# Linear attention ahead of an MLP: chunks of 64 tokens on zero-padded heads, a quartered array for the first batch, and a new order of work

## The chip, the core and the metric

The kernel runs on one core of a Trainium2 chip. The metric is the device time of one execution in microseconds. The engines are TensorE (PE; PEld is its weight load), VectorE (DVE), ScalarE (ACT), GpSimd (POOL) and SyncE (SP), which issues most DMAs.

## What is computed

A linear attention with decay over blocks of 64 tokens, then a two-layer MLP on its result. Shapes: 4 batches, 8 heads, 768 tokens, head size 64; the MLP goes from 512 to 2048 and back for 3072 tokens.

```python
for b in range(nb):                      # blocks of 64 tokens
    intra = einsum('bhic,bhjc->bhij', qb, kb) * Dmask        # lam**(i-j), i >= j
    intra = einsum('bhij,bhjd->bhid', intra, vb)
    inter = einsum('bhid,bhde->bhie', qb * lam_pow, kv_state)
    out[:, :, sl] = intra + inter
    kv_state = lam_block * kv_state + einsum('bhsd,bhse->bhde', kb * rev_pow, vb)
x = out.transpose(0, 2, 1, 3).reshape(B * S, H * D)
h = x @ w_in
g = where(h >= 1, h, where(h <= -1, 0, (h + 1) ** 2 / 4))
return g @ w_out
```

The block size may be chosen freely as long as the decay is carried along; the result is the same recurrence.

## The kernel before

The 3072 tokens are cut into eight stripes, (batch, first block of 128, number of blocks):

```python
STRIPES = [(0, 0, 4), (0, 4, 2), (1, 0, 3), (1, 3, 3), (2, 0, 3), (2, 3, 3), (3, 0, 3), (3, 3, 3)]
FORMS = "pfffwwww"
```

A stripe has four units, one for each pair of heads; L02v is the load of v for stripe 0, pair 2. Attention works in chunks of 128 tokens. A unit's work on TensorE is: transposes of k and q (T and Q, L344), scores of k against q (S, L368 or L372), k against v for the state (R, L449 or L455), and the output from masked scores and from the state before (O, L506, L513, L519, L527, L532, L538). DVE applies the mask (s, L383 or L389) and carries the state (r: a scan, L468, or step by step, L475 and L477). ScalarE, POOL and DVE cast and scale k, q and v (L295 to L320) and ScalarE evacuates PSUM (t, u, o).

The letter in FORMS says how two heads of 64 share the 128 x 128 array. In "p" (stripe 0) a matmul takes half or a quarter of the array for one head. In "f" (stripes 1 to 3) k and v lie beside zeros, kz and vc, so that the state comes out block-diagonal; scores take half the rows. In "w" (stripes 4 to 7) k is zero-padded per head, k and q are transposed by a DMA issued from SyncE (L336), and the output comes with tokens on the partitions and is transposed by another DMA (X, L557).

The MLP of a stripe is 16 tiles of the first layer (P, or K for the first three of stripe 0, one slice of the contraction at a time as soon as its pair of heads is there; L595, L609), ScalarE's ReLU (h, L618), the rest of the activation on DVE in groups of four tiles (A, L575 to L577), the second layer in four parts for each 128 rows (Y, L627), a copy (y) and a store (U). The last 128 rows are closed in two column parts (Z, L647). The weights come in eight casting DMAs issued from POOL (W0 to W7, L235 and L239).

The order of all this is written out in one string of words, ORDER. Every engine and every DMA queue executes its instructions in that order; a word such as `W0@L00q` makes a load wait for another. D1 is a dummy matmul on the identity (L583). The list before has 23 of them in the start.

Of the kernel before, what the change touches and what calls it, by code (L numbers as in the profile page):

```python
# [16 lines left out]
def _ins(ap, idx, mid):  # L17

    a = list(ap.ap)
    a = a[:idx] + [[0, mid]] + a[idx:]  # L20
    return bass.AP(ap.tensor, ap.offset, a)

FORMS = "pfffwwww"
STRIPES = [(0, 0, 4), (0, 4, 2), (1, 0, 3), (1, 3, 3), (2, 0, 3), (2, 3, 3), (3, 0, 3), (3, 3, 3)]

ORDER = """
D1 L00q D1 B0a D1 B2a D1 D1 L01q q01d D1 L03q D1 L00k L01k D1 D1 L01v D1 q00d B1a L00v D1 D1
k00a D1 D1 k01g D1 T00 Q01 T01 D1 E t00 Q00 L02k v01a u00 D1 q03d R01 D1 r01 k02g L02q D1 B3a
# [5 lines left out]
W6@L10v t11 S10 P0c L20k@W1 q13d r11 R10 h0e Q12 h0d s10 T12 S11 r10 t12 u12 s11 P0f z13a O11  # L40
S12 o11 O10 A01 z12g T13 h0c Q13 W7@L02q Y010 h0f t13 u13 h0a Y020 v12g L20q@W1 q20g Y030 Y021
s12 Y000 Y011 o10 L20v@W1 Y031 v13a A02 k21g Y001 Y022 Y032 S13 Y012 R13 A03 k20a Y013 R12
L21q@W1 b13d r13 s13 y01 z20g Y033 O13 r12 O12 y03 o13 Y023 o12 T20 P12 Y002 L21k@W7 v20g y02
Q20 q21g h12 u20 t20 P15 L30k h15 R20 P13 P10 Q21 h13 h10 u21 S20 P11 q23g P17 T21 h11 h17 r20
P16 s20 P1b t21 v21d O20 z21d k22a P14 o20 q22d R21 A10 r21 h1b L30q h14 h16 Y003 L21v z22g Q22
S21 k23g s21 P19 P1d y00 P1a T22 z23g k30g h19 A11 h1a u22 P1f T30 t22 q30g z30g L31k L31q k31g
L31v h1f U01 z31g P18 q31g Q30 P1c U00 t30 S22 Q23 h1d T23 u30 s22 P1e t23 Y100 Y101 h18 u23 A12
G40 h1c v23g T31 S23 s23 k33g v22g v33g Q31 O21 Y110 t31 o21 u31 R22 L30v Y111 v32g R23 h1e r22
r23 Y112 S30 z33d A13 q33g O22 O23 o22 s30 o23 Y102 P21 P27 h27 L40k Q33 T33 R33 Y113 u33 t33
k32g r33 P23 q32d S31 L40q y11 v31d v30g P22 R31 T32 Q32 Y103 h22 u32 t32 L40v z32g r31 P24 s31  # L50
G41 R30 R32 G42 k42g k40g h21 h23 P20 r30 S32 r32 s32 h20 h24 P25 P2a A20 q40d P29 O30 k41g h2a
y10 P2b S33 P28 O32 h2b h29 P2e o30 h28 P2c h2c s33 q41d h25 O31 A22 P26 h26 o31 P2d P2f o32 O33
Y200 h2d o33 L50q P33 h2f h2e P32 h33 P30 P31 A21 Y201 h30 T40 T41 h32 G43 P39 A23 h31 v42a v41d
Y202 P38 P3a A30 h39 q42a U03 h3a P37 R42 h37 S40 Y210 v40d L50k s40 P35 R40 r42 Y211 h38 q51g
Y203 k43a P3b G50 R41 S41 y20 r40 h3b T42 v43d h35 q43g P3c k51d s41 L50v U11 q50a U20 r41 Y212
P34 O40 T43 O41 k50g Y213 U02 o40 S42 v50a P3f h34 v52g T50 X40 k52g y21 P3e R43 P3d s42 h3c o41
L60q P36 r43 S43 q53a O42 h3e Y320 h36 Y220 s43 o42 h3f A31 T51 O43 o43 Y221 R52 S50 v51a A32
Y300 Y222 h3d k53g X41 r52 Y301 X42 Y321 Y223 X43 R50 Y302 q52d Y322 P43 R51 A33 y22 P42 Y303
s50 r51 Y323 S51 v53g U10 T53 T52 r50 h43 y32 s51 L60k P47 q62g P40 O51 h42 P4a h40 S52 k60g
L60v o51 O50 h47 h4a s52 y30 q60a P4b R53 P41 P46 S53 r53 h41 q61a P45 Y310 h45 Y311 U22 k61a  # L60
k63d A40 P44 h4b O52 v62g P48 s53 q63g o50 U30 h46 h44 P49 O53 h48 P4d T60 o52 X51 T61 X50 v63a
v60g o53 P4c X52 h4c X53 Y312 Y313 S60 P4f k62d v61g y31 P4e R60 h49 Y410 A41 s60 U32 h4e Y400
A42 r60 h4d R62 h4f P53 Y411 A43 T62 r62 T63 h53 Y401 L70q q71g Y402 q73g q70g S61 U31 P51 h51
P5a Y403 Y420 R63 y40 Y421 P54 h54 s61 S62 R61 r61 r63 s62 h5a Y412 P56 L70k h56 O60 P52 L70v
U40 Y413 k70d P50 O62 h52 o60 v70g y41 k71g P5b U41 P59 h50 h5b h59 O61 P55 o61 S63 T70 P58 A50
P57 X61 Y422 h57 s63 O63 v72d h55 Y423 P5d h58 o63 k72a P5f P5c v71d A51 h5d P5e X60 o62 X63 A52
R70 R71 S70 y42 h5c Y500 Y501 X62 P61 h5f h5e T71 q72g v73g r70 P63 h63 h61 Y510 U42 T72 P62 P65
A53 R72 Y502 h65 s70 r71 P60 Y503 h62 P64 Y511 h60 k73a r72 Y512 P6d Y513 h64 S71 y50 R73 h6d
P67 A60 s71 P68 r73 O71 P6a S72 O70 o71 y51 T73 h67 s72 h68 P66 P69 h6a O72 P6b X71 S73 P6e h69
P6c s73 o70 h66 h6b Y520 U21 A62 O73 o72 X72 h6c Y521 X70 o73 A61 P6f h6f X73 Y522 Y610 Y600  # L70
Y601 Y523 h6e P70 Y611 y52 P73 h73 Y602 P72 Y612 h70 A63 P71 Y603 Y613 h71 P76 y60 h72 P79 U50
y61 h79 P78 P75 P77 h78 h75 U52 h77 P74 A70 P7d h76 P7b h74 P7a P7e h7b h7a U51 A71 h7e Y620 P7f
# [5 lines left out]
def order(ns):  # L78
    return ORDER.split()
# [663 lines left out]
```

## Time and profile before

| | us |
|---|---|
| median of 3 runs (lowest, highest) | 220.63 (220.22, 220.96) |
| span of the profiled execution | 219.9 |
| TensorE busy in it | 209.4 |
| DVE, ACT, POOL busy | 148.9, 125.4, 60.9 |

The profiled execution has no other time than its span; the runs are timed without a profile. In the time line a row gives the start, the length of a merged group, the engine, line, operation, operands and count; a matmul's length contains its way through the array, so that the distance between two starts is what it costs in a row of others.

### The profile page before, as it was taken

The numbers are of one execution on the slowest core, as the hardware profiler recorded it, in microseconds if no ns is written. First come the engines' busy times: TensorE is split into PE (matmuls) and PEld (weight loads), VectorE is DVE, ScalarE is ACT, GpSimd is POOL, SyncE is SP. The second block draws the span as 40 slices with busy tenths as digits, with TensorE's granted clock in tenths as the row PEclk, the third lists the DMA queues.
The fourth block names the chain that finished last, engine by engine and source line by source line (L and its number), as shares of the span: only waits on it lengthen the run. The fifth ranks groups of instructions, "written<-read, shape, count | busy, mean of one in ns | idle before, by whom it ended". The sixth has DMA issues, their size and how long they took to land.

```text
span 219.9 us, 4417 instructions
## 1 busy us (share of the span) xinstructions
PE 209.4 (95%) x1667; PEld 121.0 (55%) x1667; DVE 148.9 (68%) x239; ACT 125.4 (57%) x268; POOL 60.9 (28%) x122
## 2 busy tenths in 40 slices
PE   7488999999998999999999999999999999999994
PEld 2246445446765566555655666456655565555443
DVE  1387177971998789998499489936898649346700
ACT  3675689327983576874832686326655383256320
POOL 4376036007499810430311045003600000000000
PEclk9999999999999999999999999999999999999999
DMA  4999999999999993849999999899944222310103
GB/s 123 238 233 203 206 215 191 176 221 219 232 276 231 214 192 74 206 84 255 165 202 163 167 256 151 164 243 224 210 96 97 54 66 57 145 74 23 50 22 121
DMA packets 100629, 35.95 MB, mean 163 GB/s; under 512 B 89216, under 2 KB 97664, under 8 KB 100608
## 3 DMA queue, kind: packets, MB, share of 16 engines
q1 hardware_dynamic: 96384, 31.47, 69.0%
q0 software_dynamic: 4224, 4.19, 12.2%
q8 instruction: 13, 0.21, 0.4%
q14 instruction: 8, 0.07, 0.1%
HBM read 27.27 MB, written 6.29 MB: 153 GB/s over the span
## 4 chain that ended last, share of the span: by engine, by line
PE 85%; SPq 5%; DMA 5%; ACT 2%; issue 1%; POOL 1%; DVE 0%; DVEq 0%; ACTq 0%
PE ph L595 36%; PE py L627 34%; SPq L164 3%; DMA v_nat<-in_v_dram 3%; PE ps L368 2%; DMA xT<-xn 2%; PE pk L449 2%; PE py L647 2%; PE po L506 2%; PE pt L344 1%; PE ps L372 1%; PE ph L609 1%; PE po L513 1%; PE po L532 1%; SPq L166 1%; SPq L160 1%
## 5 line engine op out<-in xcount | busy, mean ns | idle before, releaser
L618 ACT ACTIVATE tt<-ph,one 128x384 bf16<-128x384 f32 (+2 forms) x128 | 70.5, 584 | 41.1 <-PE ph L595 29.5
L595 PE MATMUL ph<-xT,w_in_sb 128*128 128x384 bf16 (+2 forms) x500 | 93.1, 325 | 0.5 <-DMA xT<-xn 0.5
L627 PE MATMUL py<-w_out_sb,gT 128*128 128x512 bf16 x368 | 87.7, 379 | 0.0
L595 PEld LDWEIGHTS <-w_in_sb 128*128 128x128 bf16 x500 | 46.5, 98 | 30.5 <-issue 0.2
L627 PEld LDWEIGHTS <-gT 128*128 128x128 bf16 x368 | 34.5, 98 | 35.0 <-DVE sz L477 0.8
L389 DVE TENSOR_TENSOR sc<-ps,mask 128x768 bf16<-128x768 f32 (+1 forms) x28 | 25.6, 914 | 11.9 <-PE ps L368 11.6
L576 DVE TENSOR_TENSOR tt<-tt,mm 128x1536 bf16<-128x1536 bf16 (+2 forms) x32 | 32.6, 1019 | 1.1
L577 DVE TENSOR_TENSOR gT<-tt,mm 128x1536 bf16<-128x1536 bf16 (+2 forms) x32 | 32.0, 998 | 1.2
L575 DVE TENSOR_SCALAR mm<-tt 128x1536 bf16<-128x1536 bf16 (+2 forms) x32 | 19.7, 616 | 18.5 <-ACT tt L618 17.7
L315 POOL TENSOR_SCALAR kq<-k_nat,dec 128x192 bf16<-128x192 f32 (+2 forms) x36 | 19.6, 556 | 24.9 <-DMA k_nat<-in_k_dram 24.8
L635 ACT COPY osb<-py 128x512 f32<-128x512 f32 x23 | 13.5, 585 | 20.4 <-PE py L627 16.0
L320 POOL TENSOR_TENSOR kq<-q_nat,dec 128x384 bf16<-128x384 f32 (+1 forms) x15 | 13.2, 891 | 28.5 <-DMA q_nat<-in_q_dram 15.2
L477 DVE SCALAR_TENSOR_TENSOR sz<-sz,lam_blk,pk 128x128 bf16<-128x128 bf16 x48 | 16.4, 347 | 3.5 <-PE pk L449 2.2
L297 POOL CAST vc<-v_nat 128x384 bf16<-128x384 f32 (+1 forms) x15 | 9.3, 629 | 31.6 <-DMA v_nat<-in_v_dram 15.6
L344 PE MATMUL pt<-ident,kq 128*128 128x128 bf16 x96 | 9.4, 220 | 3.2 <-ACT kq L311 2.4
L548 ACT CAST xn<-po 128x384 bf16<-128x384 f32 x16 | 7.7, 478 | 5.3 <-PE po L532 5.2
L550 ACT CAST xT<-po 128x384 bf16<-128x384 f32 (+2 forms) x16 | 7.5, 483 | 5.5 <-PE po L527 3.6
L475 DVE CAST sz<-pk 128x128 bf16<-128x128 f32 x12 | 3.4, 285 | 10.0 <-PE pk L449 10.0
L344 PEld LDWEIGHTS <-kq 128*128 128x128 bf16 x96 | 6.5, 98 | 6.6 <-ACT kq L311 2.9
L295 ACT CAST vc<-v_nat 128x512 bf16<-128x512 f32 (+2 forms) x9 | 4.9, 549 | 8.9 <-DMA v_nat<-in_v_dram 8.9
L352 ACT COPY kqT<-pt 128x384 bf16<-128x384 bf16 (+2 forms) x16 | 7.7, 482 | 2.6 <-PE pt L344 2.6
L583 PE MATMUL pw<-ident 128*128 128x512 bf16 x23 | 7.5, 450 | 1.4 <-POOL ident masks.py:199 1.4
(79 smaller groups left out, 163.0 us busy)
## 6 DMA issues: line engine op xcount, KB each, us to landing
out_dram<-osb SPq DMA_DIRECT2D x23, 256.0 KB, 3.0
q_nat<-in_q_dram SPq DMA_DIRECT2D x18, 256.0 KB, 4.5
k_nat<-in_k_dram SPq DMA_DIRECT2D x24, 128.0 KB, 4.7
v_nat<-in_v_dram SPq DMA_DIRECT2D x24, 128.0 KB, 4.4
k_nat<-in_k_dram SPq DMA_DIRECT2D x12, 256.0 KB, 4.9
v_nat<-in_v_dram SPq DMA_DIRECT2D x12, 256.0 KB, 5.1
w_in_sb<-in_moe_w_in_dram POOLq DMA_DIRECT2D x4, 512.0 KB, 9.3
w_out_sb<-in_moe_w_out_dram POOLq DMA_DIRECT2D x4, 512.0 KB, 9.1
```

The costliest lines, as they stand in the source:

```text
L315: nc.gpsimd.tensor_scalar(dst[:, hi, :, :], src[:, hi, :, :], dec[:, row, 2 * hp + hi:2 * hp + hi + 1], 0.0, AX.mult, AX.add)
L320: (nc.gpsimd if eng == "g" else nc.vector).tensor_tensor(dst, src, decay(row, 2 * hp, C, inner), op=AX.mult)
L344: nc.tensor.transpose(out=d["pt"][:, i, c, :], in_=d["kq"][:, i * C + c, :], identity=ident)
L389: nc.vector.tensor_tensor(out=d["sc"][:, :, 0:C, :], in0=d["ps"][:, :, 0:T].rearrange("p h (c i) -> p h c i", c=C), in1=_ins(mask[:, 2 * h ...
L477: nc.vector.scalar_tensor_tensor(out=d["ss"][:, c, :], in0=prev, scalar=lam_blk[:, hp:hp + 1], in1=kv, op0=AX.mult, op1=AX.add)
L575: nc.vector.tensor_scalar(mm, tt, 0.5, 1.0, AX.mult, AX.min)
L576: nc.vector.tensor_tensor(tt, tt, mm, op=AX.subtract)
L577: nc.vector.tensor_tensor(g[:, 4 * a:4 * a + 4, 0:T], tt, mm, op=AX.mult)
L595: nc.tensor.matmul(ph[:, 0:T], lhsT=w_in_sb[:, ko, ni * 128:(ni + 1) * 128], rhs=x_tiles[s][:, ko, 0:T], start=(ko == 0), stop=(ko == KO - 1))
L618: nc.scalar.activation(out=t_tiles[s, ni // 4][:, ni % 4, 0:T], in_=p_tiles[s, ni][:, 0:T], func=AF.Relu, bias=one[:, 0:1])
L627: nc.tensor.matmul(y_tiles[s, m], lhsT=g_tiles[s][:, ko, m * 128:(m + 1) * 128], rhs=w_out_sb[:, ko, :], start=(ko == 0), stop=(ko == FO - 1))
L635: nc.scalar.copy(out=osb, in_=y_tiles[s, m])
```

## The change

In FORMS, stripes 0 and 1 become "e" and stripes 2 to 7 "g", and chunks become 64 tokens.

In "e", k and v of one head lie on partitions 0 to 63 and of the other on 64 to 127, and every attention matmul but the transpose of q takes a quarter of the array for one head. Two neighbouring tokens lie beside each other on a partition, so that a read of k or v is 512 B long instead of 256 B. The state of stripe 0 is still kept per 128 tokens.

In "g", k (kq), v (vz) and the states (sz) are copied into zero-padded tiles, two copies each, one for each half of the partitions. S, R, I (the part of the output from the scores, a word of its own now) and O run on the full array with 64 columns each. The state is one scan a unit, with the state of the stripe before merged in by a matmul on the identity (L506 of the new kernel). The output comes with features on the partitions, so X and its DMA transposes go; k and q are transposed by DMA in all these stripes. v carries the decay that k carried before.

Loads of k and v are issued per unit and per head. PSUM is four banks for the MLP and four for attention. The weights' slices are 3, 4, 4 and 5 tiles of the first layer; W0 waits for L03k, W1 for L03q, W2 for L03v, W3 for W0, and the second layer's for L13q, W3, W4 and W5. The list has no dummy matmuls. It ends `Y713 y70a F72 U70 y71a U71`, where F is the former Z. Unit 00's loads of q and v, and lam, go out on ScalarE's queue. The MLP's own functions compute as before.

The core of the diff:

```diff
-FORMS = "pfffwwww"
+FORMS = "eegggggg"
+NKN, NQN, NKQ, NVZ, NSZ = 4, 3, 5, 5, 4
...
+            for h in range(2):                                   # load of k or v
+                o = t[h * HD:(h + 1) * HD, 0:n, :]
+                i = src[b, 2 * hp + h, tok, :]
+                if fm == "e":
+                    ins.append(issue(out=o.rearrange("p (b c) d -> p b (c d)", c=2),
+                                     in_=i.rearrange("(b p c) d -> p b (c d)", p=HD, c=2)))
+                else:
+                    ins.append(issue(out=o, in_=i.rearrange("(c p) d -> p c d", p=HD)))
...
+    def att_s(u, pool):
...
+                        nc.tensor.matmul(d["ps"][c][p, b * BLK:(b + 1) * BLK],      # "e"
+                                         lhsT=kT[p, j * HD:(j + 1) * HD],
+                                         rhs=qT[p, b * BLK:(b + 1) * BLK], start=True, stop=True)
...
+        for c in range(2 * C):                                                       # "g"
+            nc.tensor.matmul(d["ps"][0][:, c * HD:(c + 1) * HD], lhsT=kqT[:, c, :],
+                             rhs=qT[:, c * HD:(c + 1) * HD], start=True, stop=True)
...
+        if not first:                                                                # R, "g"
+            p = st[s - 1, hp]["ss"]
+            nc.tensor.matmul(pk[:, :, 0], lhsT=ident, rhs=p[:, :, p.shape[2] - 1],
+                             start=True, stop=True)
+        for c in range(ns - i):
+            nc.tensor.matmul(pk[:, :, i + c], lhsT=kq[:, c, :], rhs=d["vs"][:, c, :],
+                             start=True, stop=True)
...
+    def att_c(u, h, eng):
...
+        copy(eng, d["sz"][p, 0:n, p], d["ss"][p, :, 0:n].rearrange("p e c -> p c e"))
...
+        for c in range(n):                                                           # I, "g"
+            nc.tensor.matmul(po[:, c * HD:(c + 1) * HD], lhsT=d["vz"][:, c, :],
+                             rhs=d["sc"][:, 0, c * HD:(c + 1) * HD],
+                             start=(c == 0), stop=(first and c == 0), skip_group_check=True)
...
+        for c in range(int(first), 2 * C):                                           # O, "g"
+            nc.tensor.matmul(d["po"][:, c * HD:(c + 1) * HD], lhsT=d["sz"][:, c - first, :],
+                             rhs=d["qT"][:, c * HD:(c + 1) * HD],
+                             start=False, stop=True, skip_group_check=True)
```

A stretch of the new list, from the end of stripe 0's attention (`W0@L03k` and `W1@L03q` stand before it):

```text
... O00 S02am W2@L03v u03a Zk2d R02a o00a I01a s020 v03g O01 r02 o01a S03aa s021 W3@W0 L10k@W0
K00 s030 R03a L10q s031 K01 L10v r03 I02a L11k O02 I03a k102g o02a O03 ...
```

903 lines of the change are left out of this document (454 added, 449 removed).

## Prediction

> **What bounds the kernel now.** I read the page first, then busy time by stretch, then the time line of TensorE, and last the views of single groups and queues.
>
> ```profile
> PE 209.4 (95%) x1667; PEld 121.0 (55%) x1667; DVE 148.9 (68%) x239; ACT 125.4 (57%) x268; POOL 60.9 (28%) x122
> ```
>
> ```profile
> 0.00:20.50 20.50, 14.28 (x161) 8.07 (x161) 11.11 (x23) 12.62 (x27) 12.18 (x40) 1.00 1.05 199
> 20.50:217.10 196.60, 195.14 (x1510) 112.91 (x1506) 137.49 (x217) 112.76 (x242) 48.67 (x82) 1.00 0.80 161
> 217.10:219.90 2.80, 0.00 (x0) 0.00 (x0) 0.27 (x1) 0.00 (x0) 0.00 (x0) 0.87 0.28 94
> ```
>
> The page shows TensorE at 95%. The stretches (columns: length, then PE, PEld, DVE, ACT, POOL, granted clock, DMA share, GB/s) say what that is made of: 20.5 us of start, 196.6 us in which TensorE never rests, 2.8 us of tail. So the time after is a start, plus TensorE's work from the first MLP matmul on, plus its waits, plus a tail. Engines off that line matter only if they begin to hold TensorE up.
>
> A busy PE is not its pace, since matmuls overlap; the pace is the distance between starts of neighbouring groups on its time line.
>
> ```profile
> 96.96 0.34 PE L449 MATMUL pk<-vc,kq 128*128 128x64 bf16 x6
> 97.14 0.50 PE L368 MATMUL ps<-kqT 128*128 128x128 bf16 x6
> 97.47 1.03 PE L627 MATMUL py<-w_out_sb,gT 128*128 128x512 bf16 x4
> 98.33 0.81 PE L595 MATMUL ph<-xT,w_in_sb 128*128 128x384 bf16 x4
> 98.98 0.34 PE L449 MATMUL pk<-vc,kq 128*128 128x64 bf16 x6
> ```
>
> ```profile
> 54.87 0.34 PE L372 MATMUL ps<-kqT 64*128 64x128 bf16 x6
> 55.14 1.05 PE L595 MATMUL ph<-xT,w_in_sb 128*128 128x256 bf16 x8
> 56.02 0.33 PE L344 MATMUL pt<-ident,kq 128*128 128x128 bf16 x3
> ```
>
> ```profile
> 18.50 0.41 PE L455 MATMUL pk<-vc,kq 128*64 128x64 bf16 x8 [0.52 <-ACT vc L295]
> 18.85 0.40 PE L372 MATMUL ps<-kqT 64*128 64x128 bf16 x8
> 19.17 0.41 PE L519 MATMUL po<-sc,vc 128*64 128x128 bf16 x8
> 19.52 0.40 PE L538 MATMUL po<-kqT,ss 64*64 64x128 bf16 x6
> 19.84 0.41 PE L519 MATMUL po<-sc,vc 128*64 128x128 bf16 x8
> ...
> 20.51 0.82 PE L609 MATMUL ph<-xT,w_in_sb 128*128 128x512 bf16 x3
> 21.26 0.41 PE L519 MATMUL po<-sc,vc 128*64 128x128 bf16 x8
> ```
>
> On the full array: 64 columns 0.18/6 = 0.030 us, 128 columns 0.33/6 = 0.055, 256 columns 0.88/8 = 0.110, 384 columns 0.65/4 = 0.1625, 512 columns 0.86/4 = 0.215. A change between full and split array costs about 0.10: three matmuls of L609 take 0.75 where 3 x 0.215 = 0.645. Quartered ones (64*64, L538): 0.32 for six, less 0.10, is 0.037 each; in longer runs I expect the pace of L455 (0.35 less 0.10, over eight, 0.031). Bounds: 0.031 and 0.053 (0.32/6).
>
> **TensorE's work from the first MLP matmul on.** The MLP is untouched: 384 x 0.1625 + 64 x 0.110 + 64 x 0.215 + 368 x 0.215 + 3.5 (L647: 16 of 384, 16 of 128 columns) = 166 us. Instruction counts below come from the loops of the code.
>
> Before, stripes 1 to 7: 292 matmuls of 128 columns (transposes, ps, po) x 0.055 = 16.1; 224 of 64 columns x 0.030 = 6.7; ps of the f stripes in 12 groups of 0.27 and 0.10 back, the four short ones 0.05 less, 4.2. Sum 27.0. With 0.7 left over from stripe 0, 193.7 of the 196.6 us; 2.9 us are waits and the last matmul's drain.
>
> After, stripes 2 to 7: no transposes on TensorE, and chunks of 64 tokens halve the score matrix. 144 (S) + 144 (R with its merge) + 144 (I) + 132 (O) = 564 of 64 columns x 0.030 = 16.9. Stripe 1: 128 quartered x 0.031 = 4.0, 8 transposes of q 0.4, six visits to the quartered array at two changes each 1.2. Sum 22.5, so 4.5 us saved. Against that, R03, I02, O02, I03 and O03 now stand behind the first MLP matmul: 60 x 0.031 and four changes, 2.3 instead of 0.7. Work after: 166 + 22.5 + 2.3 = 190.8, a net saving of 2.9. At the upper bound of the quartered pace 188 x 0.022 = 4.1 us more.
>
> **The start.** Before, the first MLP matmul stood at 20.5 us, behind stripe 0's last casts. After, it waits for W0, for stripe 0's unit 0, and for 8.7 us of TensorE work ahead of it (220 quartered x 0.031, 16 transposes of q x 0.055, some nine changes).
>
> ```profile
> 8.35 1.13 SPq L164 DMA_DIRECT2D k_nat<-in_k_dram  x2
> ```
>
> ```profile
> 13.24 2.45 POOL L235 DMA_DIRECT2D w_in_sb<-in_moe_w_in_dram  x3
> ```
>
> ```profile
> DMA to landing us min/median/max: 6.9/9.3/10.7
> ```
>
> ```profile
> 1.43 4.73 PE L583 MATMUL pw<-ident 128*128 128x512 bf16 x15 [1.43 <-POOL ident masks.py:199]
> ```
>
> A load costs SyncE about 0.55 us. Stripe 0 needs 17 issues there (three more go out on ScalarE's queue) instead of 20, and W0's release, L03k, is the 13th: issued at 8, landed near 12. On POOL, W0 stands behind q00, q02 and q03 (0.9 to 1.2 us each, late loads) and 20 small memsets, so about 12.3 instead of 13.24. It is three quarters of a former slice: 5 to 6.9 us to landing, 17.3 to 19.2. I take 17.5. Behind W0 on POOL wait W1, v02's and v03's scaling and W2; behind L10k, which waits for W0 on SyncE, all further loads. The reads of 512 B shorten the queue ahead of W0; how much is open between nothing (SyncE's issue sets the pace) and some 3 us, and I count nothing.
>
> The dummy matmuls (L583) are gone. The first 15 took 4.73 us where 15 x 0.215 = 3.2 would do at full clock: about 1.5 us lost to a slow clock before it rises. Now real work pays that; from the first key cast, estimated at 6.3 us, to 17.5 there are 11.2 us for 8.7 of work, which covers it. Without that cover the start is 19.
>
> **The other engines.** Copies of k, v and the states into padded tiles are new, the 16 DMA transposes of outputs and 16 of ScalarE's evacuations of transposes go.
>
> ```profile
> L320 POOL TENSOR_TENSOR kq<-q_nat,dec 128x384 bf16<-128x384 f32 x14 | 12.6, 911 | 28.5 <-DMA q_nat<-in_q_dram 15.2 <-DVE gT L577 10.2 <-DMA kqT<-kq 3.2
> L297 POOL CAST vc<-v_nat 128x384 bf16<-128x384 f32 x13 | 8.5, 665 | 21.2 <-PE po L513 12.3 <-DMA v_nat<-in_v_dram 5.2 <-PE po L532 1.5
> L415 POOL COPY kz<-kq 128x384 bf16<-128x384 bf16 x6 | 4.2, 705 | 2.8 <-ACT kq L311 2.7
> ```
>
> ```profile
> L383 DVE SCALAR_TENSOR_TENSOR sc<-ps,dec,causal 128x512 bf16<-128x512 f32 x8 | 5.6, 740 | 0.2
> ...
> L468 DVE TENSOR_TENSOR_SCAN ss<-lam_z,pk 128x256 bf16<-128x256 f32 x4 | 2.6, 677 | 4.3 <-PE pk L455 4.3
> ```
>
> POOL per unit of stripes 2 to 7: q 0.91, scaling of v 0.7, on average 1.2 copies of k and 0.45 of v 1.1, two copies of the state 1.4 (no row for 64 partitions; L415 is nearest): 4.1, 16.5 us a stripe. A stripe lasts 64 x 0.1625 + 48 x 0.215 + 4 x 0.73 = 23.6. DVE gives up one mask of 128x768 and three state steps a unit and gets a mask of 128x384 (0.55 to 0.74 by L383) and a scan of 384 columns (0.68 to 1.02 by L468): no more than before. POOL more than doubles, from 61 to about 125 us, but fits if it need not wait.
>
> The new wait on the path: O of a unit needs R, the scan, then both state copies, 0.2 + 1.0 + 1.4, and the list gives it some 4 us of other TensorE work. Behind O on TensorE wait all MLP matmuls. S to I has about 2 us for a mask of 0.6. I charge 1.1 us above the 2.9 of now: waits 4.0.
>
> **The tail.** The list issues the last two rows' stores (U70, U71) after both parts of the closing block, and SyncE keeps order.
>
> ```profile
> 216.63 1.10 SPq L656 DMA_DIRECT2D out_dram<-osb  x2
> ```
>
> ```profile
> 217.08 0.29 DVE L654 COPY osb<-py 128x128 f32<-128x128 f32 x1 [8.08 <-PE py L647]
> ```
>
> ```profile
> out_dram<-osb SPq DMA_DIRECT2D x23, 256.0 KB, 3.0
> ```
>
> Before, the last store went out at about 217.4 and was small. After it, two of 256 KB follow: 0.4 us each to issue and up to 3.0 to land. Tail 4.7 instead of 2.8.
>
> **Sum.** 17.5 + 190.8 + 4.0 + 4.7 = 217.0 against the profiled span of 219.9. The runs' median, 220.63, lies 0.7 above that span; the forecast is 217.7.
>
> **Rivals.** *POOL and DVE hold each other up (slower).* POOL operations stretch beside DVE's tensor-tensor ones, and these beside POOL's:
>
> ```profile
> 61.20 1.01 POOL L320 TENSOR_TENSOR kq<-q_nat,dec 128x384 bf16<-128x384 f32 x1
> 62.15 0.96 POOL L415 COPY kz<-kq 128x384 bf16<-128x384 bf16 x1
> ```
>
> ```profile
> 61.55 1.21 DVE L576 TENSOR_TENSOR tt<-tt,mm 128x1024 bf16<-128x1024 bf16 x1
> ```
>
> ```profile
> L576 DVE TENSOR_TENSOR tt<-tt,mm 128x1536 bf16<-128x1536 bf16 x24 | 23.9, 996 | 0.8
> ```
>
> Here 1024 columns take 1.21 us, where 1536 take 0.996 on average. If the two exclude each other wholly, a stripe needs 16.5 on POOL and at least 4 x 2 x 0.996 = 8.0 on DVE (more with the third step of the activation): 24.5 or more against 23.6. It decides once POOL's share passes about 15.6 a stripe or a unit's O waits over 0.12 us on average. With 0.3 us of wait in each of 24 units, 7.2 us more: 225. For it: the rows above, and state copies queued behind casts that wait for loads. Against: the means already contain such waits, and POOL also works while DVE reads PSUM. Chance 0.21. [...]
>
> *Early loads rule (about equal).* Window one moved 199 GB/s at a DMA share of 1.05: DMA is full. W2, the w_out chain and stripe 2 now hang on each other (W0 to W3 to W5 to W7, L20k behind W4), while TensorE asks for stripe 2 about 5 us sooner. Two waits of 1.5 to 2 us: 221. Chance 0.17.
>
> *Quartered pairs don't overlap their weight loads (slower).* At 0.053 each: 4.1 us after the first MLP matmul and about 2 us in the start: 224. Against: L455's 0.031. Chance 0.07. [...] L538 at 0.037 to 0.053 leaves it open.
>
> *More than forecast.* Start at 16.5, waits as now, tail 4: 214.9. Chance 0.12.
>
> **Numbers.** Forecast 0.43. Faster by over 0.3% (about what a measurement here can tell from no change): 0.43 + 0.12 + a quarter of the second rival, 0.59. Same 0.07, slower 0.34. The range runs from below the best case, 213.5, to the third rival's 224. The likeliest case's own range is 215 to 220.
>
> **What would show it.** The first L629 at 17 to 19 us; groups of six 64-column matmuls 0.18 apart; groups of sixteen quartered ones in about 0.5; POOL near 125 us; three to five us of PE waits after the start; a last store issued 1.1 us after TensorE's end. I am wrong if PE waits for state copies or masks sum to over 6 us, if the start passes 20, or if quartered groups take 0.8.

## The result, and the profile after

The changed kernel takes 257.48 us (median of 4 runs, 255.99 to 260.05) against 220.43 us (220.05 to 220.96) for the kernel before on the same chip: the ratio is 1.166, 95% interval 1.161 to 1.171. Medians take all runs; the ratios here and below leave out runs more than 1.5% above the fastest of their kernel. The forecast was 217.7 us in a range of 213.5 to 224.0, so the kernel is 17% slower where 1% faster was expected. The span of the profiled execution is 254.3 us.

Lines of the page after: the span, the engines' busy time, the chain of work that ended last by engine, and the group of the state copies. The second fence has that chain in the kernel before.

```profile
span 254.3 us, 5012 instructions
PE 213.4 (84%) x1889; PEld 125.2 (49%) x1908; DVE 146.8 (58%) x190; ACT 136.3 (54%) x268; POOL 131.9 (52%) x209
...
PE 33%; DMA 32%; POOL 19%; SPq 6%; issue 4%; DVE 2%; POOLq 1%; ACT 1%; ACTq 1%
...
L339 POOL COPY sz<-ss 64x320 bf16<-64x320 bf16 (+1 forms) x48 | 41.9, 875 | 20.4 <-DVE ss L528 18.8
```

```profile
PE 85%; SPq 5%; DMA 5%; ACT 2%; issue 1%; POOL 1%; DVE 0%; DVEq 0%; ACTq 0%
```

TensorE is busy hardly longer than before (213.4 against 209.4 us), but in a span that is 34 us longer, and the chain, which was 85% TensorE's, is now to a third DMA.

Busy time by stretch (length, PE, PEld, DVE, ACT, POOL, granted clock, DMA share, GB/s), first before, then after:

```profile
0.00:10.00 10.00, 5.54 (x27) 2.36 (x28) 2.98 (x10) 5.24 (x12) 3.75 (x18) 1.00 0.84 177
10.00:20.00 10.00, 8.24 (x130) 5.36 (x129) 7.62 (x12) 6.88 (x15) 8.16 (x22) 1.00 1.26 221
20.00:30.00 10.00, 10.00 (x68) 4.71 (x65) 4.32 (x8) 7.19 (x14) 0.59 (x3) 1.00 1.20 216
30.00:40.00 10.00, 10.00 (x79) 5.30 (x78) 7.10 (x14) 9.24 (x25) 5.27 (x10) 1.00 1.14 187
...
60.00:160.00 100.00, 98.82 (x841) 59.64 (x839) 81.00 (x131) 59.10 (x128) 36.37 (x61) 1.00 0.99 192
```

```profile
0.00:10.00 10.00, 1.30 (x22) 1.02 (x23) 4.52 (x16) 2.99 (x6) 8.48 (x40) 1.00 0.84 163
10.00:20.00 10.00, 9.04 (x183) 8.00 (x184) 7.59 (x12) 7.14 (x15) 6.48 (x12) 1.00 0.94 173
20.00:30.00 10.00, 4.42 (x106) 3.17 (x101) 3.57 (x6) 2.03 (x4) 1.90 (x4) 0.93 1.20 204
30.00:40.00 10.00, 8.71 (x75) 4.30 (x78) 1.90 (x3) 5.48 (x11) 5.69 (x13) 0.73 0.57 139
...
60.00:160.00 100.00, 84.97 (x735) 50.59 (x741) 62.56 (x73) 63.61 (x131) 75.60 (x99) 0.98 0.91 186
```

Read the last two columns first. Before, the DMA engines were full (share 1 and more) from 10 to 40 us; after, they are less busy from 10 to 20 us and half idle from 30 to 40 us. By 40 us 6.8 MB have been moved instead of 8.0 (the GB/s of four rows by 10 us each), and in the long stretch behind the rate is no higher than before (186 against 192 GB/s), so nothing is made up. TensorE loses 6.9 us between 20 and 40 us and 13.9 us between 60 and 160 us.

Where the chain of waits passes through the start and into stripe 2 (start, length, what):

```profile
9.30 6.24 DMA q_raw<-in_q_dram
...
15.70 1.06 POOL qn L370
16.77 4.90 DMA w_in_sb<-in_moe_w_in_dram
...
22.32 7.77 DMA k_raw<-in_k_dram
...
40.55 5.34 DMA w_out_sb<-in_moe_w_out_dram
...
48.53 11.36 DMA q_raw<-in_q_dram
```

The last cast of stripe 0's q on POOL waits for a load that lands at 15.5 us; W0 stands behind it and is issued at 16.77 us instead of the predicted 12.3. At 21.67 us W0 lands, which releases L10k; stripe 1's first keys then take 7.8 us more. W4 lands at 45.9 us, which releases L20k, and stripe 2's q lands at 59.9. On TensorE's time line, below, stripe 1's transposes (L431) start at 31.1 us, behind a rest of 6 us, and further on the new R stands beside I and O:

```profile
21.94 0.59 PE L629 MATMUL ph<-xT,w_in_sb 128*128 128x512 bf16 x2 [0.80 <-DMA w_in_sb<-in_moe_w_in_dram]
...
31.07 0.42 PE L431 MATMUL pt<-ident,kn 64*64 64x64 bf16 x8 [5.85 <-POOL kn L339]
...
101.70 0.34 PE L560 MATMUL po<-sc,vz 128*128 128x64 bf16 x6
101.88 0.34 PE L580 MATMUL po<-kqT,sz 128*128 128x64 bf16 x6
...
104.92 0.49 PE L510 MATMUL pk<-vs,kq 128*128 128x64 bf16 x6 [1.19 <-POOL vs L387]
105.22 0.36 PE L467 MATMUL ps<-kqT 128*128 128x64 bf16 x6
```

I costs 0.18 us for six (101.70 to 101.88), as forecast; R costs 0.30 (104.92 to 105.22). Its outputs go to every sixth or seventh column of PSUM. TensorE's largest waits, in total, times and longest (the second line is the wait ahead of TensorE's first instruction):

```profile
PE po L580 <- POOL sz L339: 8.9, 6, 3.7
PE pt L431 <- ACT kn L337: 7.4, 1, 7.4
PE pt L431 <- POOL kn L339: 5.8, 1, 5.8
PE pk L510 <- POOL vs L387: 4.5, 4, 2.2
PE ps L467 <- DMA kqT<-kq: 2.9, 4, 2.1
```

Read alone, this list blames POOL's state copies. The experiments show that they are a smaller part.

### The profile page after: what moved, and what is told of

Same layout as the page of the kernel before. It is cut to its first block, busy times and chain, and to the rows that moved or that the text cites. A ratio compares the mean times of both kernels' runs of the same rounds, so it can differ in the third digit from the quotient of the medians.

```text
span 254.3 us, 5012 instructions
## 1 busy us (share of the span) xinstructions
PE 213.4 (84%) x1889; PEld 125.2 (49%) x1908; DVE 146.8 (58%) x190; ACT 136.3 (54%) x268; POOL 131.9 (52%) x209
## 4 chain that ended last, share of the span: by engine, by line
PE 33%; DMA 32%; POOL 19%; SPq 6%; issue 4%; DVE 2%; POOLq 1%; ACT 1%; ACTq 1%
PE py L645 17%; DMA k_raw<-in_k_dram 12%; PE ph L617 11%; DMA q_raw<-in_q_dram 9%; POOL sz L339 7%; DMA kqT<-kq 5%; POOL kq L370 4%; POOL vs L387 3%; POOL kq L339 3%; DMA v_raw<-in_v_dram 3%; SPq L220 2%; DMA w_out_sb<-in_moe_w_out_dram 2%; DMA w_in_sb<-in_moe_w_in_dram 2%; PE py L661 1%; PE pk L510 1%
## 5 line engine op out<-in xcount | busy, mean ns | idle before, releaser
L645 PEld LDWEIGHTS <-gT 128*128 128x128 bf16 x368 | 35.1, 99 | 38.5 <-issue 1.6
L339 POOL COPY sz<-ss 64x320 bf16<-64x320 bf16 (+1 forms) x48 | 41.9, 875 | 20.4 <-DVE ss L528 18.8
L482 DVE SCALAR_TENSOR_TENSOR sc<-ps,dec,causal_g 128x384 bf16<-128x384 f32 x24 | 14.6, 613 | 38.2 <-PE ps L467 38.2
L605 DVE TENSOR_TENSOR tt<-tt,mm 128x1536 bf16<-128x1536 bf16 (+2 forms) x32 | 35.5, 1111 | 1.1
L528 DVE TENSOR_TENSOR_SCAN ss<-lam_z,pk 128x384 bf16<-128x384 f32 (+1 forms) x28 | 25.2, 906 | 16.4 <-PE pk L510 14.6
L337 ACT CAST vz<-v_raw 64x384 bf16<-64x384 f32 x37 | 18.8, 508 | 24.5 <-DMA v_raw<-in_v_dram 23.6
L387 POOL TENSOR_SCALAR vs<-v_raw,dec 128x384 bf16<-128x384 f32 (+2 forms) x36 | 23.4, 653 | 10.6 <-DMA v_raw<-in_v_dram 5.9
L337 ACT COPY osb<-py 128x512 f32<-128x512 f32 (+1 forms) x24 | 13.7, 579 | 28.3 <-PE py L645 16.3
L370 POOL TENSOR_TENSOR kq<-q_raw,dec 128x384 bf16<-128x384 f32 x24 | 21.7, 905 | 13.5 <-DMA q_raw<-in_q_dram 12.2
L339 POOL CAST kq<-k_raw 64x384 bf16<-64x384 f32 x28 | 17.5, 623 | 18.0 <-DMA k_raw<-in_k_dram 11.4
L337 ACT CAST kq<-k_raw 64x384 bf16<-64x384 f32 x20 | 10.2, 510 | 16.5 <-DMA k_raw<-in_k_dram 10.6
L510 PE MATMUL pk<-vs,kq 128*128 128x64 bf16 x132 | 11.5, 243 | 4.5 <-POOL vs L387 4.5
L431 PE MATMUL pt<-ident,kn 64*64 64x64 bf16 x96 | 4.0, 231 | 13.3 <-ACT kn L337 7.4
```

Source lines behind the costliest of these rows:

```text
L337: nc.scalar.copy(out=o, in_=i)
L339: (nc.gpsimd if eng == "g" else nc.vector).tensor_copy(o, i)
L370: (nc.gpsimd if eng == "g" else nc.vector).tensor_tensor(o, raw[s, hp, "q"][:, :, 0:C, :], f, op=AX.mult)
L387: (nc.gpsimd if eng == "g" else nc.vector).tensor_scalar(o, i, f, 0.0, AX.mult, AX.add)
L482: nc.vector.scalar_tensor_tensor(out=d["sc"][:, c, 0:T].rearrange("p (n i) -> p n i", n=n), in0=d["ps"][c][:, 0:T].rearrange("p (n i) -> p ...
L528: nc.vector.tensor_tensor_scan(d["ss"].rearrange("p e c -> p (e c)"), lam_z[ns, fm][:, hp, :], d["pk"].rearrange("p e c -> p (e c)"), 0.0, ...
```

## The experiments

Kernels whose names begin with a are variants of the changed kernel, with b of the kernel before. Each was timed beside the kernel before on the same chip (medians of 220.3 to 220.9 us). Median us, and the ratio to before:

| kernel | us | ratio, 95% interval |
|---|---|---|
| changed kernel | 257.5 | 1.166 (1.161 to 1.171) |
| a_ungate | 248.8 | 1.129 (1.124 to 1.135) |
| a_wide | 247.5 | 1.125 (1.120 to 1.130) |
| a_wide_ungate | 241.2 | 1.093 (1.090 to 1.097) |
| a_wide_ungate_v_act | 247.5 | 1.119 (1.111 to 1.128) |
| a_one | 243.0 | 1.097 (1.090 to 1.104) |
| a_one_ungate | 234.4 | 1.061 (1.054 to 1.068) |
| a_one_ungate_o_free | 230.0 | 1.042 (1.040 to 1.045) |
| a_one_ungate_flat | 232.7 | 1.055 (1.052 to 1.059) |
| a_all | 227.4 | 1.032 (1.030 to 1.033) |
| a_o_free | 257.9 | runs from 254.0 to 262.0 |
| a_no_c | 253.6 | 1.149 (1.144 to 1.154) |
| a_pkflat | 257.8 | 1.171 (1.168 to 1.174) |
| a_v_act | 259.2 | 1.172 (1.162 to 1.181) |
| a_rows256 | 260.5 | 1.181 (1.175 to 1.188) |
| b_no_dummies | 222.2 | 1.008 (1.005 to 1.010) |
| b_halves | 242.6 | 1.100 (1.098 to 1.103) |
| b_split | 236.5 | 1.071 (1.067 to 1.075) |
| b_merge | 226.5 | 1.025 (1.020 to 1.030) |

**a_ungate.**

```diff
-... W3@W0 L10k@W0 ... W6@W4 L20k@W4 ...
+... W3@W0 L10k ... W6@W4 L20k ...
```

> The changed kernel without two words of its list: L10k no longer waits for W0, and L20k no longer waits for W4; everything else stands. Theory GATES: the new list holds loads back while the DMA engines idle (share 0.35 between 33 and 42 us), so stripe 1's first keys come at 31 and stripe 2's at 57 us; then the early waits fall (6.0 us at the first transpose of stripe 1's keys, about 4 us around 59 us with the slow clock behind them) and the time drops by 6 to 10 us from 257.5. Rival HALVES: the loads are late because each goes to 64 partitions; then the loads only trade places with the weights' slices, W0 lands later by as much as stripe 1 comes earlier, and the time moves by less than 2 us. Rival POOL: nothing but the first 30 us changes, 2 to 4 us.

8.7 us came back, within theory GATES' bounds of 6 to 10. From 30 to 40 us the DMA share is 0.90 instead of 0.57. Both gates were placed so that weights come first; TensorE needed stripe 1's keys and stripe 2's q more.

**a_wide.**

```diff
-            o = t[h * HD:(h + 1) * HD, 0:n, :]
+            o = t[:, h * C:(h + 1) * C, :]
...
-                    in_=i.rearrange("(b p c) d -> p b (c d)", p=HD, c=2)))
+                    in_=i.rearrange("(b p c) d -> p b (c d)", p=128, c=2)))
...
-                ins.append(issue(out=o, in_=i.rearrange("(c p) d -> p c d", p=HD)))
+                ins.append(issue(out=o, in_=i.rearrange("(c p) d -> p c d", p=128)))
```

> The changed kernel with each load of k and v spread over 128 partitions: two DMAs a unit as before, the same bytes and the same rows (512 B in stripes 0 and 1, 256 B after), but every DMA fills all 128 partitions with half of the columns. The tokens then lie in the wrong places, so attention's values are not the reference's; the work and the order are unchanged. Theory HALVES: what makes the loads slow is that a DMA with 64 partitions uses a part of the DMA engines or ports; then 128 KB of stripe 0 land every 0.5 us or less instead of 0.65, the last load of stripe 0 lands before 17.5 us instead of 18.6, the median issue to landing of k and v of stripes 2 to 7 drops from 2.8 to about 2.3 us, and the time falls by 6 to 15 us. Rival ISSUE: SyncE's 0.60 us a load sets the pace and the shape does not matter: less than 2 us. Rival GATES or POOL: stripe 0 earlier, but the total by less than 3 us.

10.0 us came back. The start, of the changed kernel and then of a_wide:

```profile
4.00:12.00 8.00, 3.21 (x56) 2.69 (x56) 5.07 (x13) 4.03 (x10) 5.91 (x20) 1.00 1.16 222
...
16.00:20.00 4.00, 4.00 (x99) 3.73 (x97) 2.82 (x6) 2.19 (x5) 3.95 (x6) 1.00 0.58 92
```

```profile
4.00:12.00 8.00, 4.46 (x88) 3.87 (x88) 6.32 (x14) 5.30 (x13) 7.17 (x22) 1.00 1.11 313
```

The DMA engines are full in both (share over 1), but the same loads (k and v in rows of the same 512 B, q unchanged) come at 313 GB/s with k and v on 128 partitions and at 222 on 64. In the start the rate went with the shape, as theory HALVES had it. Its reason, that a DMA with 64 partitions uses a part of the engines or ports, was not shown: the shares are 1.16 and 1.11. Stripe 0's last load lands at 14.4 instead of 18.6 us, W0 is issued at 13.94 instead of 16.77, and the first activation of stripe 1 starts at 61.1 instead of 66.3 us: 5.2 of the 7.0 us between the two profiled executions. From stripe 2 on, where the rows have 256 B, the issue rows differ, of the changed kernel and then of a_wide (ns minimum/median/maximum of the issuing instruction, first and last start in us):

```profile
L220 SPq DMA_DIRECT2D v_raw<-in_v_dram x48: 595/624/2052, 52.7 to 178.9; - x48
```

```profile
L220 SPq DMA_DIRECT2D v_raw<-in_v_dram x48: 432/487/1623, 49.5 to 166.7; - x48
```

The same 96 KB keep SyncE 0.62 us when they go to 64 partitions and 0.49 when they go to 128. So here the issue time went with the shape as well, which rival ISSUE took as given. The median from issue to landing of k's loads fell only from 2.8 to 2.7 us, so HALVES does not show for rows of 256 B.

**b_halves and b_split**, the question of shape and number in the kernel before: all loads of k and v cut in two, by partitions or by heads (by chunks in stripe 0).

```diff
-        return [nc.sync.dma_start(out=t[:, :, c, :], in_=src[c]) for c in range(C)]
...
+            pairs = [(t[:, :, c, :], src[c]) for c in range(C)]
...
+        return [nc.sync.dma_start(out=o[a:a + 64], in_=i[a:a + 64]) for o, i in pairs for a in (0, 64)]     # b_halves
...
+        return [nc.sync.dma_start(out=o[:, a:a + n], in_=i[:, a:a + n]) for o, i in pairs for a in (0, n)]  # b_split
```

> The kernel before, every load of k and v cut into two DMAs of 64 partitions each; the same bytes, the same 256 B rows, the same places. Theory HALVES: two DMAs onto 64 partitions move fewer bytes a microsecond than one onto 128; the start and the loads of stripes 2 to 4, where the DMA share is over 1, get later, and the time rises by 4 to 12 us, by at least 3 us more than in the kernel that cuts the same loads by heads. Rival ISSUE: only the 70 more issues on SyncE at 0.55 us cost something, the same as in the cut by heads.

> The kernel before, every load of k and v cut into two DMAs of half of the heads (of half of the chunks in stripe 0), each still on 128 partitions: the control for the cut by partitions. Theory HALVES: 0 to 4 us, what 70 more issues at 0.55 us on SyncE cost where SyncE has waits of some 50 us to spare after 60 us. Rival ISSUE: as much as the cut by partitions.

b_halves costs 22 us, b_split 16: more than theory HALVES had (4 to 12 and 0 to 4). The difference of 6 us is the shape's, the 16 us are the price of the number. Issue rows of b_halves and of b_split:

```profile
L170 SPq DMA_DIRECT2D k_nat<-in_k_dram x72: 595/617/1356, 2.7 to 170.3; - x72
```

```profile
L171 SPq DMA_DIRECT2D k_nat<-in_k_dram x72: 368/469/2139, 2.7 to 163.5; - x72
```

and the first 20 us, of b_halves and of b_split:

```profile
0.00:10.00 10.00, 6.91 (x23) 2.49 (x23) 3.88 (x10) 5.15 (x12) 3.13 (x17) 1.00 0.54 138
10.00:20.00 10.00, 6.61 (x49) 3.22 (x51) 2.79 (x4) 3.29 (x7) 3.75 (x6) 0.54 0.51 119
```

```profile
0.00:10.00 10.00, 7.03 (x33) 2.99 (x33) 3.88 (x10) 5.26 (x12) 4.27 (x18) 1.00 0.63 157
10.00:20.00 10.00, 5.22 (x69) 2.88 (x66) 5.66 (x9) 5.35 (x11) 3.42 (x5) 0.98 0.78 149
```

The DMA engines are not full (shares of 0.51 to 0.78), while SyncE issues one load behind the other (the first of v goes out at 6.9 and 8.1 us, behind eight of k from 2.7 us on): 64 KB in 0.47 us is 140 GB/s, 64 KB in 0.62 us is 106, where the kernel before moved 221. By this estimate the issue time bounds the loads here. With the first MLP matmul at 34.2 us (b_split) and 38.5 (b_halves) instead of 20.5, most of the loss is in the start; b_halves also has a granted clock of 0.54 there. The changed kernel's stripe 0 is not in this place: its engines are full, and 128 KB in 0.60 us is 218 GB/s. Its stripe 1 is: loads of 64 KB issued without a rest from 32.6 to 39.7 us at a share of 0.38. From stripe 2 on 96 KB in 0.62 us is 159 GB/s, but the share is 0.91 between 60 and 160 us, and no run shows that the issue bounds the loads there.

In the start the shape shows, with 222 GB/s against 313. Later it does not: in the stretch from 60 to 160 us a DMA share of 0.91 moved 186 GB/s in the changed kernel, 0.99 moved 192 in the kernel before. a_wide (10.0 us less on 128 partitions), b_halves and b_split (22 and 16 us more for loads cut in two) speak against the change's loads, and the prediction weighed neither their shape nor, from stripe 1 on, their number.

**a_rows256.**

```diff
-            if fm == "e":
-                ins.append(issue(
-                    out=o.rearrange("p (b c) d -> p b (c d)", c=2),
-                    in_=i.rearrange("(b p c) d -> p b (c d)", p=HD, c=2)))
-            else:
-                ins.append(issue(out=o, in_=i.rearrange("(c p) d -> p c d", p=HD)))
+            ins.append(issue(out=o, in_=i.rearrange("(c p) d -> p c d", p=HD)))
```

> The changed kernel with the loads of k and v of stripes 0 and 1 in rows of 256 B instead of 512 B, each still on 64 partitions; the tokens then lie in other places than the code takes them for, so the values of these stripes are not the reference's. The number of DMAs and bytes is the same. Theory ROWS: rows of 512 B are what the start gains: with 256 B stripe 0's last load lands 1 to 3 us later than 18.6 us, and the time is 1 to 4 us longer. Rival HALVES: 64 partitions or SyncE's issue set the pace and the row length does not matter: within 1 us.

3.0 us longer: theory ROWS. The rows of 512 B did bring something, also onto 64 partitions. In the first 20 us the rate is 138 and 178 GB/s with a share of 0.89 and 1.15, against 163 and 173 with 0.84 and 0.94: here the rows of 512 B took less of the DMA engines' time per byte.

**a_v_act.**

```diff
-L20v ... L73v
+L20va ... L73va
```

> The changed kernel with the loads of v of stripes 2 to 7 issued on ScalarE's DMA queue instead of SyncE's, at the same places of the list. Theory SYNC LOOP: from 60 to 165 us SyncE is never free: some 72 loads at 0.6 us, 18 transposes at 1.4 us and 27 us of waits of those transposes for POOL's padded keys, queries and states; the loads stand behind the transposes, POOL waits for the loads, and the next transpose for POOL. With half of the loads taken out of this line they come earlier, the 20 us that the MLP falls behind between 60 and 165 us shrink by a third or more, and the time falls by 8 to 15 us. Rival HALVES alone (the two halves land slowly whoever issues them): less than 3 us. Rival: ScalarE is in order as well and its evacuations now wait behind the loads' buffers, 0 to 5 us longer.

No gain (1.7 us longer, within the spread): theory SYNC LOOP's price was wrong. Between 60 and 160 us the DMA share rose from 0.91 to 1.16, but the rate only from 186 to 191 GB/s. The last load of v is issued 5 us earlier (174.0 instead of 178.9 us), but ScalarE now stands behind loads, and TensorE waits for what ScalarE owes:

```profile
PE py L645 <- DVE gT L606: 7.6, 4, 5.7
...
PE py L645 <- ACT tt L637: 3.7, 1, 3.7
```

**a_wide_ungate and a_wide_ungate_v_act**: the edits above together.

> The changed kernel with both edits that gained: each load of k and v on 128 partitions (tokens in the wrong places, so the values are not the reference's) and no gates on L10k and L20k. Theory SUPPLY: the time is the landing of the last load plus 72 to 77 us of work that is left then (254.3 against 181.7 us in the changed kernel, 246.1 against 173.8 without the gates, 247.3 against 170.1 wide), and each edit brings loads forward for a reason of its own: the last load at 162 to 166 us, 237 to 242 us in all, the two gains of 10.0 and 8.7 nearly adding up. Rival: both fill the same hole of 30 to 42 us, and the second gives less than 3 us: 245 or more.

> As the kernel with wide loads and without gates, and v of stripes 2 to 7 issued by ScalarE. With narrow loads this shift gained nothing: the DMA share rose over 1.1 at the same 190 GB/s. Theory SYNC LOOP behind HALVES: once the DMA engines move the wide loads faster, the issue and the transposes' waits on SyncE are next, and taking v off it gains 4 to 10 us more. Rival: 200 GB/s is what the DMA engines give for rows of 256 B in any shape, and the time stays within 2 us of the kernel with SyncE alone.

The two gains add up to 16.3 of 18.7 us, as SUPPLY had it. v on ScalarE makes it some 6 us longer (medians 241.2 and 247.5), which neither the theory (4 to 10 us gained) nor the rival (within 2 us) had. The rate between 60 and 160 us stayed near 200 GB/s, as the rival said (199 and 197). TensorE now waits 5.3 us for ScalarE's activations and evacuations (3.2 for tt, 2.1 for osb), which it did not before. The issuing time taken off SyncE was then ScalarE's: in a_v_act its 48 issues of v take 0.60 us each in the median, where SyncE's took 0.62 in the changed kernel.

**a_one and a_one_ungate**: one load for each tile, in stripe 0 with rows of 1 KB.

```diff
+            if h:
+                break
...
+                    out=t[:, 0:n, :].rearrange("p (h c) d -> p h (c d)", h=2),
+                    in_=src[b, 2 * hp:2 * hp + 2, tok, :].rearrange("h (p c) d -> p h (c d)", c=C)))
...
-                ins.append(issue(out=o, in_=i.rearrange("(c p) d -> p c d", p=HD)))
+                ins.append(issue(out=t[:, 0:n, :], in_=src[b, 2 * hp + c0 // C].rearrange("(c p) d -> p c d", p=128)))
```

> The changed kernel with one DMA for each unit's k and one for its v, on 128 partitions, in place of two of half the size: 90 loads instead of 154, the same bytes (192 KB a DMA from stripe 2 on; stripe 0 in rows of 1 KB). Tokens lie in the wrong places, so the values are not the reference's. Theory COUNT: what the loads cost is their number; 72 more of them on SyncE cost the kernel before 16 us (0.22 us each), and 64 fewer here give back 12 to 16 us beyond the 10 of the wide loads: 232 to 236 us. Rival SHAPE: the wide loads have all that there is to gain, 246 to 248 us. Rival GATES: with two gates left the early holes stay, 240 to 244 us.

> The same with the gates on L10k and L20k taken away as well. Theory COUNT: the last load lands before 155 us as in the kernel before, and the time is 226 to 232 us; the waits left on TensorE are those for the state copies and for w_out, some 15 us. Rival SHAPE: as the kernel with wide loads and no gates, 240 to 242 us, with the last load at 163 us.

a_one gives 4.4 us over a_wide, a_one_ungate 6.8 us over a_wide_ungate. Both are between the theories: the number counts, but less than COUNT's 0.22 us a load (6.8 us for 64 loads is 0.11); the price of b_split was mostly one of its start. The gain of a_one_ungate over a_wide_ungate arises between the first activations of stripes 0 and 1 (25.3 and 53.3 us, against 24.2 and 59.7), so stripe 0's longer rows, not tried apart, are not where it lies. In a_one_ungate:

```profile
10.00:20.00 10.00, 7.87 (x193) 6.68 (x189) 9.64 (x15) 6.42 (x13) 7.96 (x14) 1.00 1.18 280
20.00:30.00 10.00, 9.36 (x124) 5.13 (x126) 2.03 (x5) 5.51 (x12) 8.16 (x18) 1.00 1.20 212
30.00:40.00 10.00, 10.00 (x120) 5.38 (x115) 9.47 (x14) 8.02 (x17) 1.55 (x2) 1.00 1.25 223
...
60.00:160.00 100.00, 92.83 (x807) 53.72 (x805) 68.72 (x77) 63.70 (x130) 80.80 (x99) 0.98 1.07 203
```

The DMA engines are full again, the last load is issued at 145.6 us (150.6 in the kernel before), and the time is 23 us lower than the changed kernel's. This is the part of the miss of 40 us that the loads made, by shape, gates and number. What is left on TensorE is the next bound:

```profile
PE po L580 <- POOL sz L339: 6.6, 5, 2.2
```

**a_o_free, a_no_c and a_one_ungate_o_free**: what the state copies cost, with late and with early loads.

```diff
-            nc.tensor.matmul(d["po"][:, c * HD:(c + 1) * HD], lhsT=d["sz"][:, c - first, :],
+            nc.tensor.matmul(d["po"][:, c * HD:(c + 1) * HD], lhsT=d["vz"][:, c - first, :],
```

> The changed kernel with the O matmuls of stripes 2 to 7 reading the unit's padded v tile where they read the padded states: the state copies are still made on POOL, but nobody waits for them (the output is without the right contribution of earlier chunks). Theory POOL: TensorE's 9 us of waits for the state copies are the price of the copies; then the time falls by 8 to 12 us. Rival SUPPLY: POOL is itself late by its waits for loads, and the next unit's padded keys and values hold TensorE up instead; then the time falls by 2 to 4 us only.

> The changed kernel without the 48 state copies on POOL; the O matmuls of stripes 2 to 7 read the unit's padded v tile instead of the states, so the contribution of earlier chunks is not the reference's. It takes 42 of POOL's 132 us away, where the kernel in which nobody waited for the copies kept them. Theory POOL: POOL's queue is what holds the transposes, and through them the loads, back; without the copies the time falls by 12 us or more. Rival SUPPLY (halves, SyncE's issues and gates): POOL only waits longer for its loads, 3 us or less. Between the two: both are links of one loop, 4 to 10 us.

> The same, and O of stripes 2 to 7 reads the padded v tile, so that nobody waits for the state copies (they are still made). In the changed kernel this gained nothing, 0.2 us to the median, because the loads were late anyway. Theory POOL SECOND: once the loads are early, the waits for state copies (8.8 us in the kernel with wide loads and no gates) are the bound, and the time falls by 5 to 9 us against the kernel with one load a tile and no gates. Rival: POOL's queue is late as a whole, and TensorE waits for its keys and queries instead, 0 to 2 us.

With late loads a_o_free shows no clear gain: the median did not move, in runs that spread over 8 us; two of the four (254.0 and 255.3) lie below the changed kernel's lowest, so some 2 us are not excluded. TensorE waits there 4.9 us for the padded v instead. Without the copies at all it is 3.8 us, at the edge between the rivals of that expectation, though 42 us of POOL's work are gone. With early loads O's freedom gives 4.4 us, with intervals well apart, a little under theory POOL SECOND's 5 to 9. So the rival of the prediction, POOL's copies on the path, is real and costs some 4 us, not 40. The largest line in the list of waits is not worth its 8.9 us: take it away, and other waits stand in its place.

**a_pkflat, a_one_ungate_flat and a_all.**

```diff
-            nc.tensor.matmul(pk[:, :, i + c], lhsT=kq[:, c, :], rhs=d["vs"][:, c, :],
+            nc.tensor.matmul(pf[:, (i + c) * HD:(i + c + 1) * HD], lhsT=kq[:, c, :], rhs=d["vs"][:, c, :],
```

a_all also has the words `c..0g` as `c..0a`.

> The changed kernel with the chunk states of stripes 2 to 7 written by TensorE to 64 adjacent columns of PSUM instead of to every sixth (or seventh) one; the scan reads the tile as before, so the states are not the reference's. Theory STRIDE: a matmul of 64 columns into strided PSUM starts every 56 ns where S, I and O take 29; then these groups fall to 0.18 us for six and the time by 3 to 4 us. Rival: the groups get shorter, but the time saved turns into waits for loads and POOL, 0 to 1.5 us.

> The kernel with one wide load a tile and no gates (234.4 us), with the chunk states of stripes 2 to 7 written to adjacent PSUM columns (the scan reads them as before, so the states are not the reference's either). With late loads this edit gained nothing. Theory STRIDE: 132 matmuls at 56 instead of 29 ns, 3.6 us of TensorE's own time, which comes back now that TensorE seldom waits for loads: 230 to 232 us. Rival: TensorE comes to the state copies earlier and waits for them longer: 233.5 or more.

> The same as the last, and the copy of the first head's states moved from POOL to ScalarE (24 of 48 copies). This asks what the changed arithmetic would be worth with its loads on time. By the prediction's sum (TensorE's work 190.8 us, waits 4, tail 4.7) and a start of 20.6 us it would be 220 to 221 us, no faster than before. Theory: the copies' waits (6.6 us) fall by half or more, 226 to 229 us. Rival: ScalarE's evacuations are held up by the copies as they were by the loads of v, no gain or a loss: 230 to 234 us.

The pace did change, in a_one_ungate_flat:

```profile
92.70 0.34 PE L511 MATMUL pk<-vs,kq 128*128 128x64 bf16 x6
```

0.34 us for the group instead of 0.49. With late loads that brings nothing (the rival); with early ones 1.8 us in the medians, but the intervals overlap, so the size is not settled. The rival's longer waits for the copies do not show (5.3 us instead of 6.6). With the copies shared out the time falls by another 5.3 us to 227.4 us, as the theory had it. In a_all TensorE waits for few things:

```profile
PE py L646 <- DVE gT L607: 3.3, 4, 1.6
PE ph L630 <- DMA w_in_sb<-in_moe_w_in_dram: 2.8, 1, 2.8
...
PE po L561 <- DVE sc L482: 0.9, 1, 0.9
PE po L581 <- ACT sz L337: 0.8, 2, 0.4
```

Its first MLP matmul is at 21.1 us and its span 225.8 us. With all of this repaired, in part by loads that put the tokens where the padded tiles cannot use them, the changed kernel is still 3% slower than the kernel before.

**b_no_dummies and b_merge.**

```diff
-D1 L00q D1 B0a D1 B2a D1 D1 L01q ...
+L00q B0a B2a L01q ...
```

> The kernel before without its 23 dummy matmuls, nothing else changed. The prediction charged the slow clock of the start with 1.5 us and took it as covered. If the dummies matter as little as that, the first MLP matmul stays at 20.5 us and the time within 1 us of 220.4. Theory COLD START: without them the clock rises late (in the changed kernel it was full for the first time at 18.4 us, before at 4.1), and stripe 0's transposes, scores and states run at half pace: 1.5 to 3 us longer.

> The kernel before with the loads of stripes 2 and 3 made for all eight heads at once, as in stripes 4 to 7: 18 loads of 256 KB instead of 36 of 128 KB, put where the first half stood (L30v where L31v stood); values unchanged. Theory COUNT: 18 issues of 0.5 us less on SyncE and larger transfers; since TensorE waits 2 to 3 us in all there, the time falls by 0 to 2 us. Rival: the first units of a stripe now wait for all heads, and the time rises by 1 to 4 us.

Without the dummies the first MLP matmul comes at 22.2 instead of 20.5 us and the time is 1.8 us longer: COLD START, about the 1.5 us that the prediction read out of the dummies' durations. Eight matmuls of L372 take 0.53 us there at 19.19 us, and 0.32 in the kernel before at 18.85. b_merge is 5.6 us longer: its rival, and more than the 1 to 4 us that it gave. The loads saved are 14 (28 of k, v and q became 14; the expectation counted 36 and 18). TensorE now waits 2.0 and 1.3 us for a stripe's first v and q, and behind that the granted clock is 0.50 from 56.2 to 63.0 us; so fewer and larger loads are worse where the first unit has to wait for all eight heads. None of these runs beats the kernel before.

## Why the prediction was wrong, step by step

**The start (17.5 us; 21.9 measured).** The step that failed is W0's issue at "about 12.3" us, and in it L03k's "issued at 8, landed near 12". W0 went out at 16.77 us; from there the forecast held (4.9 us to landing, 5 to 6.9 taken). The 13th load was issued at 10.4 and landed at 16.5, and the last load of q, whose cast stands ahead of W0, landed at 15.5. So "A load costs SyncE about 0.55 us" was short (0.60 and gaps), and a landing took 6 us instead of 4. Both have one source, the loads onto 64 partitions, whose rate the prediction took for given: in a_wide the 13th is issued at 8.8, lands at 12.7, and W0 goes out at 13.94. The engines were full from 4 to 16 us (share 1.17); the 173 GB/s between 10 and 20 us (221 before) are an average with the hole behind, 92 GB/s from 16 to 20 us, when W0 was only just out and stripe 1's loads waited for it. "The reads of 512 B ... I count nothing" was low by 3 us in the good direction (a_rows256) and is not the cause.

The dummies' 1.5 us had the right size, and "11.2 us for 8.7 of work" was not enough: TensorE stood free for W0 only at 21.1 us. The trace's first record of the granted clock, at full, begins at 18.4 us (4.1 in the kernel before; the clock column shows 1.00 where there is no record). Sixteen matmuls of L461 take 0.85 us at 15.11 us and 0.44 at 18.84. The clock fell to half again from 28.6 to 35.4 us, behind TensorE's rest.

**The waits (4.0 us; some 33 measured).** Of 254.3 us, 21.9 are start and 4.7 tail; of the 227.7 between, 190.8 are the predicted work and 132 x 0.027 = 3.6 the slower R; 33 are waits and slow clock. The prediction charged 1.1 us, for O's wait for the copies, above the 2.9 of before. Its rival "Early loads rule" named the right chain (W0 to W3 to W5 to W7, L20k behind W4) and gave it two waits of 1.5 to 2 us. The step that failed is a term put at nothing: the loads of stripes 1 to 7 were never counted. There are 154 loads of q, k and v instead of 94 in the trace, 96 of them at 0.62 us and 24 transposes at 1.45 us on the same queue. a_wide, a_ungate and a_one_ungate gave back 10.0, 8.7 and 23.1 us: the supply of loads is the larger part of the error. Two signs that the prediction named for being wrong are there: the start passes 20 us, and the waits for state copies alone sum to 8.9, over 6.

**POOL.** 131.9 us against "about 125"; a state copy took 0.875 us, not 0.7. The wait that the first rival (225) named, O's for the copies, is real, with about 4 us. Its cause, POOL and DVE holding each other up, was not tried apart, and no run shows whether the two exclude each other. In the kernel before a copy of L415 took 0.96 us on POOL at 62.15, beside a tensor-tensor operation of DVE (L576), and 0.50 at 59.93, beside a read of PSUM (L389). In the changed kernel the tensor-tensor operations of 1536 columns took 1.12 us on DVE (L605) instead of 0.996.

**TensorE's work (190.8 us) and the tail (4.7 us).** The 64-column groups of S, I and O and the quartered matmuls ran as forecast (0.18 us for six; sixteen of L553 in about 0.47), so the third rival fell. R's term was mis-sized, 0.056 instead of 0.030 us each. In a_all, where the loads are early and R is flat, 225.8 - 21.1 - 4.7 = 200.0 us remain from the first MLP matmul to TensorE's end, with 5.0 us of listed waits (3.3, 0.9 and 0.8) in it: 195 against 190.8. By estimate 1.5 us of the difference are the clock, granted at half from 21.1 to 24.1 us (0.83 in the mean from 20 to 30 us). After the change the tail is 4.7 us:

```profile
247.72 1.87 PE L661 MATMUL py<-w_out_sb,gT 128*128 128x384 bf16 x21
...
250.33 0.92 SPq L654 DMA_DIRECT2D out_dram<-osb  x2
```

TensorE ends at 249.6 us, the last of the two stores goes out 1.2 us behind that, and the span ends at 254.3: this step was right.

What stays open: how much of the remaining 6.9 us of a_all is the start, DVE's late activation tiles or POOL and DVE holding each other up was not taken apart. Nor is it shown what bounds the changed kernel's loads between 60 and 160 us: engines, issue times and waits for buffers and transposes are all in reach. More buffers for k and v were not tried either.

## What to carry to other kernels

Where a change cuts the loads differently, count every load of every stage, its bytes, its partitions and the time of its issue, and compare bytes by issue time with the rate that the profile before shows, and look whether the engines are full: here the shape of the loads set the rate where they were (222 GB/s against 313, at shares of 1.16 and 1.11), and where they were not, the issues did by estimate (64 KB in 0.47 to 0.62 us, at shares of 0.51 to 0.78). The wait list here named the engine that was late last, not the one that made it late (8.9 us behind POOL's copies, which are worth some 4): take the suspected wait away, and look whether the time moves, before repairing it. Gates that put one transfer ahead of another are to be judged by what TensorE asks for next.

## What the runs showed that was not expected

- With the DMA engines full, from 4 to 12 us, the same loads, k and v in rows of 512 B, came at 222 GB/s with k and v on 64 partitions and at 313 on 128.
- SyncE's issue of a load of the same bytes lasts 0.62 us onto 64 partitions and 0.47 to 0.49 us onto 128, in both kernels.
- Cutting the kernel before's loads in two, without any other edit, costs 16 us of 220.
- Six matmuls of 64 columns into PSUM columns that lie apart take 0.30 us instead of 0.18, without a line in the profile that says so but the distance between two starts.
- Loads issued by a second engine brought nothing, and cost some 6 us where the loads were wide.
